# The last chunk of a fused attention and mixer kernel: its twelve stores spread over three DMA queues, its last sums and products in another order

## The chip, the cores and the metric

The kernel runs on one core of a Trainium2 chip. The metric is the device time of one execution in microseconds. Three runs of the kernel before took 278.12 us in the median (277.63 to 278.62).

The engines are named as in the profile: PE (TensorE, matmuls), DVE (VectorE), ACT (ScalarE), POOL (GpSimd) and SP (SyncE). DMAs are issued from three queues, those of SP, ACT and POOL. The profile lists SP's and ACT's as hardware queues (q1 and q10) and POOL's as a software queue (q0).

## The reference

Two layers follow each other. First comes attention with random features, for 8 batches, 8 heads, 576 positions and head size 64; then a mixer of tokens and channels with a residual:

```python
def phi(x):
    proj = np.einsum('bhsd,md->bhsm', x, omega)
    h = proj - np.sum(x * x, axis=-1, keepdims=True) / 2.0
    h = h - np.max(h, axis=-1, keepdims=True)
    return np.exp(h) / np.sqrt(m)
num = np.einsum('bhsm,bhmd->bhsd', q_p, np.einsum('bhsm,bhsd->bhmd', k_p, v))
den = np.einsum('bhsm,bhm->bhs', q_p, np.sum(k_p, axis=2))[..., None] + 1e-06
attn = num / den                                   # then laid out as x[8, 576, 512]

h = np.maximum(x.transpose(0, 2, 1) @ w_tok1, 0.0) @ w_tok2
u = x + h.transpose(0, 2, 1)
out = u + np.maximum(u @ w_ch1, 0.0) @ w_ch2       # float32, [8, 576, 512]
```

The change touches only the end of the last line, for the last 64 positions of all batches.

## The kernel before

**Work.** Each batch has 576 positions. The first 512 are handled batch by batch: attention, the token mixing, then the channel mixing (`channel_mix`, chunks 0 to 7). The 64 positions that are left of each of the 8 batches, 512 rows together, form one more chunk, chunk 8, the tail chunk. It is the last that runs through the channel mixing.

**The channel mixing of the late chunks.** Chunks 6 to 8 compute both matrix products by a scheme of seven block products instead of eight. In `channel_in_fast` the first product (`w_ch1`) is made in three parts p = 0, 1, 2 of seven small products each (line 1062). ACT and DVE copy or add partial results and apply the relu into the tile `r3`. In `channel_out_fast` the second product (`w_ch2`) follows. DVE first forms eight sums of pieces of `r3` (line 315, into the tile `S` or in place into `r3`): four steps, S1 to S4, each for a wide piece of 1024 columns and a narrow one of 512. S3 needs S1, S2 needs S1, and S4 needs S2.

**The tail chunk's last products.** There are seven products P0 to P6 (line 974), and in the tail chunk each comes in two halves, written P0.0 and P0.1 here. A half is 6 matmuls of 128 x 256. The halves accumulate in PSUM banks X (P0, P2, P4, P6, one after the other in the same bank), Y (P1) and Z (P3, then P5). After most of them DVE reads the bank and adds it to a float32 output tile `o` (the function `read`, line 963, 128 x 256): after P0 a partial sum `sA`, after P1 the finished block "11", after P2 a partial sum `s2`, after P4 `s3` and the finished block "22", after P5 the block "12" and after P6 the block "21". A product that continues in a bank waits until DVE has read it: P2 waits for `sA`, P4 for `s2`, P6 for `s3`. P2 needs the sums S2, P3 needs S1, P4 needs S3, P5 needs S4 and "22".

**The stores.** Twelve DMAs (line 1008) write the tail chunk out, 1 MB in all. "11" and "22" go out in two DMAs of 128 KB each, "12" and "21" in four DMAs of 64 KB each, one for each half j of the block and each half h of the 128 partitions. A store waits for the add that finishes its block.

**What sets the order.** Every piece of work is a job with a number. The list `ORDER` is the order in which the jobs are written out, and so the order on each engine and queue; each of them then runs strictly in order. `MOVED` says on which engine or queue a job runs where it isn't the usual one (`Planner.engine`). `SLOT` gives the buffer, PSUM banks among them, that a job takes. In the tail chunk the jobs 1357 to 1364 are the eight sums, 1365 to 1392 the products and reads, and 1393 to 1404 the twelve stores: 1393 and 1394 for "11", 1395 and 1396 for "22", 1397 to 1400 for "12", 1401 to 1404 for "21".

Before the change SP issues six of these stores, ACT five and POOL one (half of "22").

Of the kernel before, what the change touches and what calls it, by code (L numbers as in the profile page):

```python
# [72 lines left out]
]  # L73
SLOT = (
    "00010203010320452601510723430620153041112620702502331263741135100701332152700363111752044635171215600104072136510401273621522140701320204361"
# [1 line left out]
    "04517322047005311612173514326237325013271134051111260072314032102412101175140312243734612076123001643271034026270212356407101203501602731203"  # L77
    "51000022303022110212325010035101304703570352241401503037324610116010571232406752300411653700131615312021032420156003302110112723154023060401"
    "72243026013120507143162205711104320671127624033130231407036010103311726102015136272205122012050023132563724453203712351036012200643312721212"
    "0457020201451136170210500120741161405003243500210211470641212204101161421164200510731016272126007230400257120607120111261370211660"  # L80
)
MOVED = {
43: "ACT", 51: "ACT", 54: "ACT", 56: "ACT", 59: "ACT", 62: "ACT", 65: "ACT", 66: "ACT", 75: "DVE", 86: "ACT", 106: "DVE", 120: "ACT", 135: "DVE", 137:
# [4 lines left out]
"ACT", 737: "DVE", 752: "DVE", 758: "DVE", 762: "DVE", 768: "DVE", 862: "ACT", 865: "ACT", 876: "DVE", 879: "ACT", 901: "DVE", 909: "DVE", 911: "DVE",  # L88
915: "DVE", 979: "ACT", 1013: "ACT", 1027: "DVE", 1057: "DVE", 1069: "DVE", 1078: "DVE", 1088: "DVE", 1090: "DVE", 1098: "ACT", 1099: "ACT", 1100:
"ACT", 1101: "ACT", 1111: "DVE", 1154: "DVE", 1160: "ACT", 1174: "ACT", 1191: "ACT", 1205: "DVE", 1211: "ACT", 1216: "DVE", 1237: "DVE", 1246: "DVE",  # L90
1251: "DVE", 1265: "DVE", 1276: "ACT", 1278: "ACT", 1315: "DVE", 1331: "DVE", 1345: "DVE", 1353: "ACT", 1354: "ACT", 1355: "ACT", 1356: "ACT", 1393:
"ACT", 1394: "SP", 1395: "SP", 1397: "ACT", 1398: "SP", 1399: "ACT", 1400: "SP",
}


# [1139 lines left out]
```

## Time and profile before

| | |
|---|---|
| median of three runs | 278.12 us |
| the profiled execution | 278.79 us |
| its span (first to last instruction) | 277.0 us |
| PE busy | 264.7 us, 96% of the span |
| DVE busy | 225.5 us, 81% |
| ACT busy | 177.4 us, 64% |
| POOL busy | 83.4 us, 30% |

The profile is of one execution. All places in time are microseconds from the start of its span. A row of a timeline has the start, the busy time, the engine, the line, what is written and read, and a count; a "q" behind an engine marks its queue or sequencer, and in brackets stands how long the engine was idle before and what ended that.

Of a DMA the profile has three things: the stretch in which its queue issues it, the time from the start of that to the landing of the data, and the share of time in which the core's 16 DMA engines moved packets.

### The profile page before, as it was taken

To read this page: it belongs to the slowest core of one execution; us is meant where nothing else is said; L and a number is where in the kernel's file an instruction comes from. 1 tells how busy PE (TensorE), PEld (TensorE's weight loads), DVE (VectorE), ACT (ScalarE), POOL (GpSimd) and SP (SyncE) were. 2 spreads that over 40 slices of the span, in tenths; PEclk is the share of its full clock that TensorE was granted. 3 is DMA by queue.
4 is the path that set the end of the run, shared out by engine and by line. 5 is a ranking of instruction groups with operands and counts; after the bars stand their busy time and mean duration, and the time that the engine had idled before them with its cause. 6 is when DMAs were issued, how large, how long until landed. Compare 5 with 4: busy or idle time off the path is not lost.

```text
span 277.0 us, 6623 instructions
## 1 busy us (share of the span) xinstructions
PE 264.7 (96%) x2621; PEld 178.9 (65%) x2621; DVE 225.5 (81%) x475; ACT 177.4 (64%) x426; POOL 83.4 (30%) x107
## 2 busy tenths in 40 slices
PE   5679999999999999999999999999999999999993
PEld 2647546454656665666578546774597788888882
DVE  1588857748788978997899779999899979879892
ACT  2699998159896488845766485888777244352620
POOL 8497664006430490180007910332400000000000
PEclk9559999999999999999999999999999999999999
DMA  6999999998999989799909993970430151030215
GB/s 164 186 206 194 185 187 187 205 261 150 212 221 109 204 184 151 159 207 194 254 12 168 222 227 26 180 168 2 87 106 1 21 151 78 0 123 32 102 54 150
DMA packets 80623, 39.69 MB, mean 143 GB/s; under 512 B 63984, under 2 KB 76144, under 8 KB 80400
## 3 DMA queue, kind: packets, MB, share of 16 engines
q0 software_dynamic: 31696, 17.61, 43.7%
q1 hardware_dynamic: 47984, 19.70, 31.7%
q10 hardware_dynamic: 912, 1.97, 2.1%
q8 instruction: 20, 0.33, 0.5%
q14 instruction: 11, 0.09, 0.1%
HBM read 35.95 MB, written 16.52 MB: 189 GB/s over the span
## 4 chain that ended last, share of the span: by engine, by line
PE 83%; DMA 8%; DVE 3%; POOL 2%; ACT 1%; issue 1%; POOLq 0%
PE bank L974 26%; PE bank L1129 21%; PE bank L1062 10%; PE bank L829 5%; PE bank L842 4%; PE bank L1164 4%; DMA k<-in_k_dram 3%; PE bank L759 3%; DMA wc<-in_moe_w_ch_dram 3%; DMA r<-in_k_dram 3%; PE bank L792 3%; PE bank L713 2%; PE bank L725 2%; ACT qp L566 1%; DVE u L845 1%
## 5 line engine op out<-in xcount | busy, mean ns | idle before, releaser
L1129 PE MATMUL bank<-uT,wc 128*128 128x512 f16 x280 | 67.4, 379 | 0.1
L310 ACT ACTIVATE r<-bank 128x512 f16<-128x512 f32 (+1 forms) x73 | 42.5, 609 | 25.5 <-PE bank L1129 11.6
L315 POOL TENSOR_TENSOR vs<-v,vs 128x512 f16<-128x512 f16 x25 | 26.3, 1059 | 69.4 <-DVE vs L740 46.2
L1129 PEld LDWEIGHTS <-wc 128*128 128x128 f16 x280 | 25.6, 98 | 25.1 <-issue 0.6
L974 PEld LDWEIGHTS <-r 128*128 128x128 f16 x384 | 37.2, 98 | 6.4 <-issue 0.6
L566 ACT ACTIVATE qp<-bank 128x512 f16<-128x512 f32 x64 | 36.5, 623 | 7.6 <-PE bank L725 5.3
L566 ACT ACTIVATE kp<-bank 128x512 f16<-128x512 f32 x64 | 35.6, 613 | 6.1 <-PE bank L713 6.0
L736 DVE TENSOR_REDUCE km<-kp 128x8 f16<-128x1024 f16 x32 | 38.1, 1198 | 1.5 <-ACT kp L566 1.5
L974 PEld LDWEIGHTS <-S 128*128 128x128 f16 x288 | 27.4, 98 | 4.9 <-issue 1.3
L812 ACT ACTIVATE x<-bank,rc 128x64 f16<-128x64 f32 x120 | 26.9, 332 | 2.4 <-DVE rc L801 2.2
L312 DVE TENSOR_SCALAR r<-bank 128x512 f16<-128x512 f32 (+1 forms) x35 | 23.5, 672 | 4.3 <-PE bank L1062 2.2
L974 PE MATMUL bank<-wc,r 128*128 128x256 f16 x192 | 23.7, 273 | 0.0
L974 PE MATMUL bank<-T,r 128*128 128x256 f16 x192 | 23.6, 273 | 0.2 <-DVE o L963 0.2
L974 PE MATMUL bank<-T,S 128*128 128x256 f16 x192 | 23.6, 273 | 0.0
L1008 POOL DMA_DIRECT2D out_dram<-o x1 | 0.7, 667 | 74.0 <-issue 74.0
L963 DVE TENSOR_TENSOR o<-u,bank 128x512 f32<-128x512 f16 x28 | 18.9, 677 | 1.3 <-PE bank L974 0.9
L809 DVE TENSOR_TENSOR x<-bank,rc 128x320 f16<-128x320 f32 x40 | 18.7, 480 | 0.7
L845 DVE TENSOR_TENSOR u<-x,bank 128x512 f16<-128x512 f16 x28 | 17.6, 680 | 1.6 <-PE bank L842 1.4
L792 PEld LDWEIGHTS <-qp 128*128 128x128 f16 x256 | 13.6, 99 | 6.3 <-issue 0.6
L801 DVE RECIPROCAL rc<-bank 128x5 f32<-128x5 f32 x64 | 10.3, 180 | 8.8 <-PE bank L794 8.6
L315 POOL TENSOR_TENSOR vbd<-vt,vbd 128x512 f16<-128x512 f16 x6 | 6.3, 1051 | 36.8 <-DVE vbd L649 18.4
L963 DVE TENSOR_TENSOR o<-o,bank 128x512 f32<-128x512 f32 (+1 forms) x25 | 15.2, 612 | 2.3 <-PE bank L974 2.0
(151 smaller groups left out, 494.7 us busy)
## 6 DMA issues: line engine op xcount, KB each, us to landing
out_dram<-o SPq DMA_DIRECT2D x12, 512.0 KB, 3.1
q<-in_q_dram POOLq DMA_DIRECT2D x6, 576.0 KB, 8.2
wc<-in_moe_w_ch_dram POOLq DMA_DIRECT2D x4, 768.0 KB, 9.8
k<-in_k_dram POOLq DMA_DIRECT2D x6, 512.0 KB, 7.6
v<-in_v_dram POOLq DMA_DIRECT2D x6, 512.0 KB, 9.4
r<-in_q_dram POOLq DMA_DIRECT2D x4, 288.0 KB, 6.8
v<-in_v_dram POOLq DMA_DIRECT2D x4, 256.0 KB, 9.4
out_dram<-o SPq DMA_DIRECT2D x4, 256.0 KB, 4.2
```

Source lines behind the costliest of these rows:

```text
L310: nc.scalar.activation(out=out, in_=in_, func=AF.Relu)
L312: nc.vector.tensor_relu(out=out, in_=in_)
L315: (nc.gpsimd if eng == "POOL" else nc.vector).tensor_tensor(**kw)
L566: nc.scalar.activation(out=out, in_=in_, func=AF.Exp, bias=0.0, scale=1.0)
L736: nc.vector.reduce_max(out=t_km[place("km", (b, hp))], in_=kpv, axis=AX.X)
L792: nc.tensor.matmul(ps[:, k, j * 65 : (j + 1) * 65], st, s[:, i, 0 : D + 1], start=True, stop=True)
L812: nc.scalar.activation(out=to[:, j], in_=ps[:, j], func=AF.Copy, scale=rc_of()[:, j : j + 1])
L845: nc.vector.tensor_tensor(out=t_u[place("u", b)][:, j, :], in0=t_x[place("x", b)][:, j, :], in1=bank(n), op=ALU.add)
L963: nc.vector.tensor_tensor(out=o, in0=a, in1=ps, op=ALU.add)
L974: nc.tensor.matmul(ps[:, j * DH : (j + 1) * DH], a[:, cb, j * P : (j + 1) * P], w[:, cb, :], start=(bank_of(b, j0) not in held and j == j0 ...
L1062: nc.tensor.matmul(ps[:, 2 * P * t : 2 * P * t + 2 * P], a_[:, k, cb * P : (cb + 1) * P], m[:, :, k, :], start=(begin and t == 0 and k == ...
L1129: nc.tensor.matmul(ps, wc1[:, db, cb * P : (cb + 1) * P], moving(db), start=(db == 0), stop=(db == ND - 1))
```

## The change

Three tables are changed, and nothing else: the last 90 or so entries of `ORDER`, the last digits of `SLOT`, and some entries of `MOVED`. The computation stays the same.

```diff
-"ACT", 1394: "SP", 1395: "SP", 1397: "ACT", 1398: "SP", 1399: "ACT", 1400: "SP",
+1251: "DVE", ..., 1343: "DVE", 1353: "ACT", 1354: "ACT", 1355: "ACT", 1393: "POOL", 1394:
+"SP", 1395: "ACT", 1397: "POOL", 1400: "POOL", 1401: "ACT", 1402: "SP", 1403: "POOL", 1404: "SP",
```

**Stores.** POOL issues five of the twelve stores instead of one. On POOL's queue (`o_133` holds the blocks "11" and "12", `o_132` the blocks "21" and "22"; 64x2x256 is a store of 128 KB, 64x256 one of 64 KB):

```order
 L315 TENSOR_TENSOR vbd_114<-vt_93,vbd_114 128x8x64
+L1008 DMA out_dram<-o_132 64x256
 L1008 DMA out_dram<-o_132 64x2x256
+L1008 DMA out_dram<-o_133 64x2x256
+L1008 DMA out_dram<-o_133 64x256 x2
 L1230 UNCONDITIONAL_BRANCH
```

POOL's first store now is half of the first finished half of "21"; halves of "22" and "11" follow, and it ends with one store of each half of "12", the last of all among them.

SP's queue has four of the stores instead of six:

```order
 L1015 DMA out_dram<-o_132 128x1024
+L1008 DMA out_dram<-o_132 64x256
 L1008 DMA out_dram<-o_133 64x2x256
-L1008 DMA out_dram<-o_132 64x2x256
-L1008 DMA out_dram<-o_132 64x256 x2
-L1008 DMA out_dram<-o_133 64x256 x2
+L1008 DMA out_dram<-o_132 64x256
+L1008 DMA out_dram<-o_133 64x256
 L1230 UNCONDITIONAL_BRANCH
```

What moved there: the store of half of "22" went to ACT, and one store of "12" to POOL. ACT's queue has three instead of five: "22", then one of "21", then one of "12".

**Products.** The fourteen half products stand in another order. On PE, from P3 on, one row for each half product of 6 matmuls (`S_71` as the second operand marks P2, P3 and P5, `r30_130` the others; before, in the order P3.0, P3.1, P1.1, P2.0, P2.1, P1.0, P4.0, P4.1):

```order
L974 MATMUL bank2_65<-T_72,S_71 128x256
L974 MATMUL bank1_64<-T_72,S_71 128x256
L974 MATMUL bank6_69<-wc2_81,r30_130 128x256
L974 MATMUL bank7_70<-T_72,S_71 128x256
L974 MATMUL bank3_66<-T_72,S_71 128x256
L974 MATMUL bank6_69<-wc2_81,r30_130 128x256
L974 MATMUL bank7_70<-T_72,r30_130 128x256
L974 MATMUL bank3_66<-T_72,r30_130 128x256
```

After those come P6.0, P6.1, P5.1 and P5.0. Now, in the order P3.1, P3.0, P2.1, P2.0, P4.1, P4.0, P1.0:

```order
L974 MATMUL bank7_70<-T_72,S_71 128x256
L974 MATMUL bank1_64<-T_72,S_71 128x256
L974 MATMUL bank2_65<-T_72,S_71 128x256
L974 MATMUL bank3_66<-T_72,S_71 128x256
L974 MATMUL bank2_65<-T_72,r30_130 128x256
L974 MATMUL bank3_66<-T_72,r30_130 128x256
L974 MATMUL bank6_69<-wc2_81,r30_130 128x256
```

After those come P6.1, P6.0, P1.1, P5.0 and P5.1. So P1, which stood between P3 and P2 and between P2 and P4, is behind P4 with one half and behind P6 with the other, and P4 follows P2 directly.

**Sums.** DVE's order changes with it. Its rows from the narrow S1 on, before:

```order
L315 TENSOR_TENSOR S<-r_130 128x512
L315 TENSOR_TENSOR r_130<-r_130 128x4x256
L315 TENSOR_TENSOR S<-S,r_130 128x512
L963 TENSOR_TENSOR o_133<-ut,bank_66 128x256
L963 TENSOR_TENSOR o_133<-ut,bank_70 128x256
L315 TENSOR_TENSOR S<-S,r_130 128x1024
L315 TENSOR_TENSOR S<-r_130,S 128x1024
L315 TENSOR_TENSOR r_130<-r_130 128x2x256
L963 TENSOR_TENSOR o_133<-o_133,bank_69 128x256
```

Now:

```order
L312 TENSOR_SCALAR r_130<-r_130 128x2x256
L315 TENSOR_TENSOR S<-r_130 128x512
L315 TENSOR_TENSOR S<-S,r_130 128x1024
L315 TENSOR_TENSOR S<-S,r_130 128x512
L963 TENSOR_TENSOR o_133<-ut,bank_65 128x256
L315 TENSOR_TENSOR r_130<-r_130 128x2x256
L963 TENSOR_TENSOR o_133<-ut,bank_66 128x256
L315 TENSOR_TENSOR r_130<-r_130 128x4x256
L963 TENSOR_TENSOR o_133<-ut,bank_65 128x256
L963 TENSOR_TENSOR o_133<-ut,bank_66 128x256
L315 TENSOR_TENSOR S<-r_130,S 128x1024
```

Both pieces of S2 now come before the `sA` reads, the wide S3 stands between the two `sA` reads and the two `s2` reads, and S4 stands behind the `s2` reads. A relu of 512 columns (job 1356, line 312) came to DVE from ACT. Earlier in the tail chunk two more jobs changed sides: the relu of part 2 of the first product (job 1343, 512 columns from PSUM) went from ACT to DVE, and a copy of 512 columns (job 1345) from DVE to ACT. ACT's last three relus come in the order of parts 2, 1, 0, while PE makes the products that they read in the order 0, 1, 2.

More of the change, by code (lines that the diff above doesn't have):

```diff
@@ L79 @@
     "72243026013120507143162205711104320671127624033130231407036010103311726102015136272205122012050023132563724453203712351036012200643312721212"
-    "0457020201451136170210500120741161405003243500210211470641212204101161421164200510731016272126007230400257120607120111261370211660"
+    "0457020201451136170210500120741161405003243500210211470641212204101161421164200510731016272126007230400257120607120111261230711606"
 )
@@ L90 @@
 "ACT", 1101: "ACT", 1111: "DVE", 1154: "DVE", 1160: "ACT", 1174: "ACT", 1191: "ACT", 1205: "DVE", 1211: "ACT", 1216: "DVE", 1237: "DVE", 1246: "DVE",
-1251: "DVE", 1265: "DVE", 1276: "ACT", 1278: "ACT", 1315: "DVE", 1331: "DVE", 1345: "DVE", 1353: "ACT", 1354: "ACT", 1355: "ACT", 1356: "ACT", 1393:
-"ACT", 1394: "SP", 1395: "SP", 1397: "ACT", 1398: "SP", 1399: "ACT", 1400: "SP",
+1251: "DVE", 1265: "DVE", 1276: "ACT", 1278: "ACT", 1315: "DVE", 1331: "DVE", 1343: "DVE", 1353: "ACT", 1354: "ACT", 1355: "ACT", 1393: "POOL", 1394:
+"SP", 1395: "ACT", 1397: "POOL", 1400: "POOL", 1401: "ACT", 1402: "SP", 1403: "POOL", 1404: "SP",
 }
```

8 rows, old and new, of the table ORDER are left out of this document.

## The prediction

> **What bounds the kernel now.** I read the page first, then the chain of waits over the last microseconds, then the timelines of the engines and queues there, and last the transfers.
>
> ```profile
> span 277.0 us, 6623 instructions
> PE 83%; DMA 8%; DVE 3%; POOL 2%; ACT 1%; issue 1%; POOLq 0%
> ```
>
> The span is PE's to 83%. But the change starts only some 20 us before the end, so what counts is what ends last there. The chain of waits of the last 27 us closes with these pieces (start, length, what):
>
> ```profile
> 262.96 1.31 PE bank L1062 x12
> 264.27 8.02 PE bank L974 x72
> 272.28 0.02 issue
> 272.31 0.42 DVE o L963
> ```
>
> PE runs without a break until 272.3, and one add follows until 272.73. The span goes on for 4.3 us more, and these belong to the stores. On their queues:
>
> ```profile
> 270.57 0.61 SPq L1008 DMA_DIRECT2D out_dram<-o  x1
> 271.13 0.67 POOL L1008 DMA_DIRECT2D out_dram<-o  x1 [74.01 <-issue]
> 272.57 0.68 SPq L1008 DMA_DIRECT2D out_dram<-o  x1
> 272.86 0.59 ACTq L1008 DMA_DIRECT2D out_dram<-o  x1
> 273.35 0.55 SPq L1008 DMA_DIRECT2D out_dram<-o  x1
> 273.55 0.64 ACTq L1008 DMA_DIRECT2D out_dram<-o  x1
> ```
>
> Their landings, from the DMA view of three windows (KB each, us from issue to landing): the SP and the POOL store of "22", issued at 270.57 and 271.13, and ACT's last, issued at 273.55.
>
> ```profile
> out_dram<-o SPq DMA_DIRECT2D x1, 128.0 KB, 2.5
> out_dram<-o POOLq DMA_DIRECT2D x1, 128.0 KB, 3.0
> out_dram<-o ACTq DMA_DIRECT2D x1, 64.0 KB, 2.1
> ```
>
> The block that is finished at 272.73 is issued only at 273.35 and 273.55, because SP and ACT are still busy with earlier stores: the last issue is 0.82 us late. It lands at 273.55 + 2.1 = 275.7. SP's queue has waited for that landing for 1.7 us, and it then goes through its remaining semaphores:
>
> ```profile
> SPq L1230 <- DMA out_dram<-o: 1.7, 1, 1.7
> L1230 SPq EVENT_SEMAPHORE  x11: 17/28/28, 273.9 to 277.0; - x11
> ```
>
> So 277.0 - 275.7 = 1.3 us stand behind the last landing whatever lands last. The end is set by PE's last product, the add, the queues, the transfer, and this rest. The transfers themselves are not free either. Windows of one microsecond (their length, then each engine's busy time, the clock, the share of the DMA engines, GB/s):
>
> ```profile
> 270.00:271.00 1.00, 1.00 (x10) 0.77 (x9) 0.85 (x4) 0.00 (x0) 0.00 (x0) 1.00 0.83 203
> 271.00:272.00 1.00, 1.00 (x12) 0.88 (x10) 0.77 (x2) 0.00 (x0) 0.67 (x1) 1.00 0.28 86
> 272.00:273.00 1.00, 0.27 (x3) 0.00 (x0) 0.50 (x2) 0.00 (x0) 0.00 (x0) 1.00 0.84 194
> 273.00:274.00 1.00, 0.00 (x0) 0.00 (x0) 0.00 (x0) 0.00 (x0) 0.00 (x0) 1.00 0.92 258
> 274.00:275.00 1.00, 0.00 (x0) 0.00 (x0) 0.00 (x0) 0.00 (x0) 0.00 (x0) 1.00 0.87 259
> 275.00:277.00 2.00, 0.00 (x0) 0.00 (x0) 0.00 (x0) 0.00 (x0) 0.00 (x0) 1.00 0.09 25
> ```
>
> From 272 to 275 the DMA engines are busy to 84 to 92%. They stop 0.09 x 2.0 = 0.2 us past 275.0, and the landing is seen about 0.5 us later.
>
> **Part 1: sums and products.** PE does the same 84 half-product matmuls, DVE nearly the same work. These rows price it:
>
> ```profile
> 264.10 1.47 PE L974 MATMUL bank<-T,S 128*128 128x256 f16 x12
> 268.03 2.93 PE L974 MATMUL bank<-T,r 128*128 128x256 f16 x24
> 270.80 1.47 PE L974 MATMUL bank<-wc,S 128*128 128x256 f16 x12
> 261.85 0.68 DVE L1075 TENSOR_TENSOR r<-r,bank 128x512 f16<-128x512 f32 x1
> 263.57 0.69 DVE L315 TENSOR_TENSOR r<-r 128x1024 f16<-128x1024 f16 x1
> 264.17 0.42 DVE L315 TENSOR_TENSOR S<-S,r 128x512 f16<-128x512 f16 x1
> 264.51 0.74 DVE L963 TENSOR_TENSOR o<-ut,bank 128x256 f32<-128x256 f16 x2
> L312 DVE TENSOR_SCALAR r<-r 128x1024 f16<-128x1024 f16 x2 | 0.8, 422 | 0.0
> ```
>
> 72 matmuls in 8.02 us against 12 in 1.31 leave 8.02 - 6 x 1.31 = 0.16 us of waiting. It lies in the 24 matmuls from 268.03 to 270.80: 2.77 us, where 24 at the pace of the chain's 1.31/12 take 2.62. There P6 waits for the `s3` adds. In the new order P1.0 stands between P4 and P6, which gives DVE 0.65 us more, so I take these 0.15 us as gone.
>
> What could be late next is P4, which now follows P2 directly and waits for `s2`. On DVE a wide sum takes its slot for 264.17 - 263.57 = 0.60 us, a narrow one for 0.34, an add for 0.74 - 0.41 = 0.33, the relu that came to it about half of its 1024-column row and a little, 0.25. I lay the new order out from the last add of the first product, which I leave at 261.85 (its slot 0.60). S1 wide starts at 262.45, the relu at 263.05, S1 narrow at 263.34, S2 at 263.67 and 264.27, `sA` at 264.60, S3 narrow at 264.94, `sA` at 265.27, S3 wide from 265.60 to 266.29. PE, at 0.655 us for a half, starts P3.1 at 264.10 as before, P2.1 at 265.41, P2.0 at 266.07, and wants to start P4.1 at 266.72. P2.1 is done shortly before 266.27; the `s2` add then takes 0.41, to 266.68. P4.1 so waits for 0.0 to 0.1 us. The bounds are 0, and 0.6 if each add had to wait for a whole wide sum. I take 0.05, since S3 wide ends within 0.02 us of the point where the add can start. P6 and P5 then find their adds done with 0.1 us and more to spare. Sum of this part: -0.15 + 0.05 = -0.1 us; the last add ends at about 272.6.
>
> The jobs that changed sides cost nothing on the path: the relu of part 2 takes 0.60 us on DVE from about 257.3, and the add that it delays is needed only by a product at 259.7. The copy on ACT starts behind a relu that ends at 257.53 and is done before its reader's time, 258.9. ACT's last three relus end up to 0.9 us later, since ACT starts with the part that PE makes last, at about 265.9; their readers, P1.0 and S4, come at 267.2 or later. The rows of the cover:
>
> ```profile
> 256.47 1.06 ACT L310 ACTIVATE r<-r 128x1024 f16<-128x1024 f16 x1 [2.50 <-DVE r L1075]
> 258.86 0.60 PE L1062 MATMUL bank<-uTt,wc 128*128 128x256 f16 x4
> 259.74 1.47 PE L974 MATMUL bank<-wc,S 128*128 128x256 f16 x12
> 263.43 1.57 ACT L310 ACTIVATE r<-bank 128x512 f16<-128x512 f32 x3 [0.23 <-PE bank L1062]
> ```
>
> **Part 2: the queues of SP and ACT.** With seven stores instead of eleven, they no longer run late. SP's last store comes at 272.6 behind one that starts at about 272.1 and takes 0.6, so at about 272.75. At 2.1 to 2.5 us it lands by 275.3. Alone that would be worth up to 0.4 us.
>
> **Part 3: POOL's queue.** Five issues of 0.67 us. What POOL costs is seen here:
>
> ```profile
> L1008 POOLq EVENT_SEMAPHORE  x1: 76414/76414/76414, 194.2 to 194.2; - x1
> 270.13 0.42 DVE L963 TENSOR_TENSOR o<-o,bank 128x256 f32<-128x256 f32 x1
> L371 POOL DMA_DIRECT2D vt<-in_v_dram x16 | 10.8, 680 | 0.3 <-POOL vbd L315 0.3
> L390 POOL DMA_DIRECT2D k<-in_k_dram x12 | 10.2, 854 | 0.1
> ```
>
> "22" was finished at 270.55, POOL's wait ended at 194.2 + 76.4 = 270.6, and its store started at 271.13, where SP's started at 270.57: POOL wakes up 0.55 us later. But where stores or loads queue up, it issues one behind the other: 28 loads at 0.68 to 0.85 us with 0.4 us of idle time in all. So I start the five at 270.6, 271.3, 271.9, 272.6 and, whichever is later, 273.3 (five at 0.67) or 272.6 + 0.55 = 273.15. From there to landing 2.1 us at least (ACT's last, on engines that run empty) and 3.0 at most (POOL's row, twice the size). I take 2.4, nearer to ACT's because the size and the empty engines are the same and 0.5 of POOL's 3.0 is what separates it from SP's 2.5 on the same block. The last store then lands at 275.7, between 275.3 and 276.3.
>
> The Trainium skill, in "DMA: Bandwidth & Descriptors", section "Anatomy of one DMA — SWDGE (gpsimd) path", fits a POOL DMA with 2.0 us and its bytes over 436 GB/s. As an estimate by that page, 64 KB take 2.15 us and the last landing is at 275.4, 0.3 us earlier; the trace's 128 KB, at 3.0 against the page's 2.3, speak for the later value.
>
> **Part 4: the transfers.** Before, "11" was stored at 268.7, and its quarter of the megabyte had moved by 271.1 (the first two windows). Now "11" is finished near 271.3, and the whole megabyte moves from the first store on. That one is issued at about 270.05, and 1.3 us pass before its packets run (the store of 270.57 brings only a share of 0.28 to the window up to 272). The windows from 272 to 275 move 194, 258 and 259 KB, together 0.71 MB, at a mean share of 0.88, so full engines move 0.27 MB per us. 1.05 MB take 3.9 us: from 271.4 to 275.3, and 0.5 us to the landing give 275.8; what one queue alone leaves unused up to 272 comes on top, some 0.2 at most.
>
> **Sum.** Part 3 says 275.7, part 4 275.8 to 276.0, before it was 275.7. I take 275.8, +0.1 us: the queues' gain and the 0.1 us of part 1 are used up by the engines and by POOL's late start. The profiled execution would have a span of 277.1 instead of 277.0. It took 278.79, 0.7 us above the median of 278.12, so I put the difference on the median: 278.2 us. A measurement of this kernel can tell about 0.3%, 0.8 us, from no change.
>
> **Rivals.**
>
> *The queues are all that counts (gain).* For it: the last issue is 0.82 us late on two queues that are full from 270.6 on. Against it: the shares of 0.84 to 0.92. If the engines keep up and POOL lands in 2.1 us, the last landing is at 275.25, 0.45 us earlier: 277.7. For 0.3% it would have to be at 274.85, 1.7 us behind POOL's last start, which no row of a store shows. The Trainium skill, in "Perfetto Trace Analysis", section "DMA Optimizations", says for this gain that spreading DMAs over sync, scalar and GpSimd may help where issuing them is the bottleneck and not the transfer; by the shares above it is both.
>
> *POOL wakes up anew for each store (slower).* Each of the five would then cost 0.55 + 0.67 = 1.22 us, the fifth would start at 270.6 + 4 x 1.22 = 275.5, land at 277.9 with 2.4, and the time would be 2.2 us above now: 280.3. For it: in this trace no POOL DMA that waits for DVE stands right behind another; the 28 loads had little to wait for. Against it: a queue that is already busy when its wait ends shows no gap anywhere. It decides from a last start later than 274.1 (274.1 + 2.4 + 1.3 = 277.8, 0.8 above now).
>
> *POOL's own end sets the span (a little slower).* Its queue's closing instruction ran until 271.1 + 3.5 = 274.6, half a microsecond past the landing of its only store:
>
> ```profile
> L1230 POOLq DRAIN  x3: 51/93/3512, 271.1 to 276.7; - x3
> ```
>
> If that came 3.5 - 0.7 = 2.8 us behind the last issue, it would end at 274.0 + 2.8 = 276.8, where SP's chain reaches POOL at 276.3 now: 0.5 us more, 278.6.
>
> **Chances.** My forecast with its neighbours (the sum, the smaller gain, POOL's end), all within 0.3%: 0.70. POOL waking anew, in full or in good part: 0.17; other ways to lose 0.8 us (DVE's order holding PE up at several places, transfers that disturb one another): 0.06. A gain of more than 0.8 us: 0.07. So faster 0.07, same 0.70, slower 0.23. The range goes from 277.5 (the first rival with part 1's 0.15 us in full) to 279.4, where POOL pays about half of its wakes.
>
> **What would show it.** Right: PE without waits above 0.1 us from 264 to 272, the last add at 272.5 to 272.7, SP's last store issued before 272.9, POOL's five starts 0.6 to 0.75 us apart, DMA shares of 0.85 and more from 272 to 275, a last landing at 275.5 to 276.1 that is POOL's. Wrong: gaps of 0.5 us between POOL's stores, or engines that run empty before 274.5.

## The result and the profile after

The changed kernel takes 278.82 us in the median of 13 runs (278.4 to 279.63), the kernel before 278.17 us in 13 runs beside it. The ratio is 1.0020, with a 95% interval of 1.0012 to 1.0028: it is slower by 0.56 us, 0.33 to 0.78 us. The forecast was 0.1 us.

The profiled execution of the changed kernel has a span of 276.9 us, shorter than that of before. That is no gain of the change: here the whole program runs a microsecond earlier long before the change begins. POOL's long wait ahead of its first store starts at 193.1 in this trace and at 194.2 in that of before, and the start of P3 has the same lead. So the two traces are compared from the start of P3 on. Of the changed kernel, the page's first line and rows of the timelines of PE and DVE (P3 and P2; P4; the last add):

```profile
span 276.9 us, 6620 instructions
263.06 2.78 PE L974 MATMUL bank<-T,S 128*128 128x256 f16 x24
265.74 1.47 PE L974 MATMUL bank<-T,r 128*128 128x256 f16 x12
271.18 0.42 DVE L963 TENSOR_TENSOR o<-o,bank 128x256 f32<-128x256 f32 x1 [0.23 <-PE bank L974]
```

| from the start of P3 | before | after |
|---|---|---|
| start of P3 | 264.10 | 263.06 |
| to the last add's end | 8.63 us | 8.55 us |
| from there to the last landing | 2.95 us | 4.06 us |
| from there to the end of the span | 1.34 us | 1.24 us |
| start of P3 to the end | 12.92 us | 13.85 us |

So the compute part became 0.08 us shorter, and the way from the last add to the last landing 1.11 us longer. The stores of the changed kernel, each by its row on SP's and on ACT's queue, POOL's five together:

```profile
269.05 0.56 SPq L1008 DMA_DIRECT2D out_dram<-o  x1
270.32 0.65 SPq L1008 DMA_DIRECT2D out_dram<-o  x1
271.03 0.67 SPq L1008 DMA_DIRECT2D out_dram<-o  x1
271.79 1.47 SPq L1008 DMA_DIRECT2D out_dram<-o  x1
270.98 0.50 ACTq L1008 DMA_DIRECT2D out_dram<-o  x1
269.61 2.88 POOL L1008 DMA_DIRECT2D out_dram<-o  x5 [73.53 <-DVE o L963]
L1008 POOL DMA_DIRECT2D out_dram<-o x5: 544/589/642, 269.6 to 271.9; - x5
```

The queues do what the change wanted of them: the last add ends at 271.60, SP's last issue starts at 271.79 and POOL's at 271.9. The landings are another matter. The DMA view of the last stretch of the changed kernel, all twelve stores (KB each, median us from issue to landing), and then of the window that holds only the two last:

```profile
out_dram<-o POOLq DMA_DIRECT2D x2, 128.0 KB, 3.8
out_dram<-o SPq DMA_DIRECT2D x3, 64.0 KB, 3.9
out_dram<-o POOLq DMA_DIRECT2D x3, 64.0 KB, 3.5
out_dram<-o ACTq DMA_DIRECT2D x1, 128.0 KB, 2.9
out_dram<-o ACTq DMA_DIRECT2D x2, 64.0 KB, 4.1
out_dram<-o SPq DMA_DIRECT2D x1, 128.0 KB, 4.5
...
out_dram<-o SPq DMA_DIRECT2D x1, 64.0 KB, 3.9
out_dram<-o POOLq DMA_DIRECT2D x1, 64.0 KB, 3.5
```

Before, a 64 KB store took 2.7 us in the median and the last one 2.1. Now the medians of the three queues are 3.5 to 4.1, and the last to land is SP's: 271.79 + 3.9 = 275.7, behind POOL's at 275.4. SP's last issue itself took 1.47 us instead of the usual 0.6. The windows of the changed kernel, with the columns of those before:

```profile
270.00:271.00 1.00, 1.00 (x11) 0.78 (x8) 0.71 (x2) 0.00 (x0) 1.00 (x3) 1.00 0.56 131
271.00:272.00 1.00, 0.14 (x2) 0.00 (x0) 0.42 (x1) 0.00 (x0) 1.00 (x3) 1.00 0.74 165
272.00:273.00 1.00, 0.00 (x0) 0.00 (x0) 0.00 (x0) 0.00 (x0) 0.48 (x1) 1.00 0.91 218
273.00:274.00 1.00, 0.00 (x0) 0.00 (x0) 0.00 (x0) 0.00 (x0) 0.00 (x0) 1.00 0.97 301
274.00:275.00 1.00, 0.00 (x0) 0.00 (x0) 0.00 (x0) 0.00 (x0) 0.00 (x0) 1.00 0.73 231
```

The DMA engines moved 131 and 165 GB/s in the first two windows, and in the last they were at 0.73 while SP's last stores were still out.

### The profile page after: what moved, and what is told of

It reads as the page before. It is cut to its first block, busy times and chain, and to the rows that moved or that the text cites. A ratio compares the mean times of both kernels' runs of the same rounds, so it can differ in the third digit from the quotient of the medians.

```text
span 276.9 us, 6620 instructions
## 1 busy us (share of the span) xinstructions
PE 265.2 (96%) x2621; PEld 179.2 (65%) x2621; DVE 225.6 (81%) x476; ACT 176.5 (64%) x425; POOL 85.5 (31%) x111
## 4 chain that ended last, share of the span: by engine, by line
PE 55%; issue 27%; DMA 8%; POOL 4%; DVE 2%; ACT 1%; POOLq 0%
PE bank L1129 20%; PE bank L974 13%; PE bank L829 4%; PE bank L1164 4%; PE bank L842 3%; DMA k<-in_k_dram 3%; DMA r<-in_q_dram 3%; DMA wc<-in_moe_w_ch_dram 2%; PE bank L759 2%; PE bank L792 2%; PE bank L725 2%; PE bank L713 2%; ACT qp L566 1%; DVE u L845 1%; POOL vs L315 1%
## 5 line engine op out<-in xcount | busy, mean ns | idle before, releaser
L312 DVE TENSOR_SCALAR r<-bank 128x512 f16<-128x512 f32 (+1 forms) x36 | 24.3, 674 | 4.3 <-PE bank L1062 2.2
L1008 POOL DMA_DIRECT2D out_dram<-o x5 | 2.9, 587 | 73.5 <-DVE o L963 73.5
```

What stands on the lines that cost most here:

```text
L312: nc.vector.tensor_relu(out=out, in_=in_)
```

## The experiments

Each kernel was timed beside the kernel before on the same chip and profiled once. "P3 to end" is the time from the start of P3 to the end of the span in its profile, free of what happens earlier in the program. A line number can be a few off from that of before.

| kernel | ratio to before (95% interval) | P3 to end | last add to last landing | of it: until that store's issue + issue to landing | last landing to end |
|---|---|---|---|---|---|
| before | 1 | 12.92 us | 2.95 us | 0.82 + 2.13 | 1.34 |
| the change | 1.0020 (1.0012 to 1.0028) | 13.85 | 4.06 | 0.19 + 3.88 | 1.24 |
| e1: new order, old queues | 1.0003 (0.9990 to 1.0017) | 13.34 | 3.61 | 1.07 + 2.54 | 1.19 |
| e2: old order, new queues | 1.0027 (1.0013 to 1.0040) | 13.66 | 3.87 | 0.20 + 3.67 | 1.16 |
| e3: the change without "11" | 0.9989 (0.9978 to 1.0000) | 12.90 | 2.96 | 0.29 + 2.66 | 1.40 |
| e5: old order, no POOL | 0.9987 (0.9970 to 1.0004) | 12.93 | 3.01 | 0.80 + 2.21 | 1.29 |
| e6: old order, three early on POOL | 0.9975 (0.9965 to 0.9985) | 12.63 | 2.96 | 0.14 + 2.82 | 1.04 |
| e7: old order, "21" joined | 0.9986 (0.9974 to 0.9999) | 12.63 | 2.95 | 0.40 + 2.55 | 1.05 |
| e8: "21" joined, no POOL | 0.9963 (0.9951 to 0.9976) | 12.34 | 2.73 | 0.34 + 2.39 | 0.99 |
| e9: old order, three late on POOL | 0.9996 (0.9983 to 1.0009) | 13.09 | 3.42 | 0.14 + 3.28 | 1.04 |
| e10: old order, five early on POOL | 0.9997 (0.9985 to 1.0009) | 13.15 | 3.34 | 0.03 + 3.31 | 1.17 |

From the start of P3 to the last add's end it is 8.63 us in every kernel with the old order and 8.54 or 8.55 with the new one, so nearly all that differs in "P3 to end" lies behind the last add. The last store to land is one of SP's or ACT's in all of them but e3, where it is POOL's.

The order of the kernels is nearly the same by the ratio and by "P3 to end". But the timed differences from before are on average 0.3 us lower than those of the profiles (e8: -1.03 us against -0.58; the change: +0.56 against +0.93). One profile of before stands against all of them, so its tail was probably a short one; this is left open, and a difference of 0.3 us between two profiles is to be read with care.

### Order or queues

The first two kernels each make one half of the change. Edit of e1, in the tables of the changed kernel:

```diff
-... 1393: "POOL", 1394: "SP", 1395: "ACT", 1397: "POOL", 1400: "POOL", 1401: "ACT", 1402: "SP", 1403: "POOL", 1404: "SP",
+... 1393: "ACT", 1394: "SP", 1395: "SP", 1397: "ACT", 1398: "SP", 1399: "ACT", 1400: "SP",
```

> The changed order of sums and products, but the twelve stores on the queues of before (SP six, ACT five, POOL one). In the trace of the changed kernel 5.3 us pass from the last add's end to the end of the span, before 4.3 us. Theory A, the whole megabyte meets in the last 5 us because "11" is finished at the end: the tail stays at 5.0 us or more and the time is 0.5 us or more above before. Theory B, POOL's five stores are what is slow: the tail is back at 4.3 to 4.6 us and the time within 0.2 us of before, or 0.1 us under it, since the last add comes 0.1 us earlier.

e2 has the reverse edit in the kernel before.

> The order of before, with "11" stored at 268.7, but the stores on the queues of the change (POOL five). Theory A: 768 KB are left for the end as before, the tail is 4.3 to 4.6 us and the time within 0.2 us of before. Theory B: POOL's stores slow the transfers here as well, the tail is 4.9 us or more and the time 0.5 us above before.

Measured: from the last add's end to the end of the span 4.80 us in e1 and 5.03 us in e2, P3 to end 0.42 and 0.74 us above before, timed +0.1 and +0.75 us. The queues are the greater half, and alone they cost as much as the whole change within the intervals: theory B for the most part. But theory A is not empty: in the profile the new order alone brings the last landing 0.57 us later behind the start of P3 (e1). What the new order leaves for the end can be counted in the trace. These are the packets from the last add's end to 276, of before, e2, e1 and the changed kernel:

```profile
DMA packets 682, 0.63 MB, mean 193 GB/s; under 512 B 144, under 2 KB 656, under 8 KB 682
DMA packets 539, 0.63 MB, mean 156 GB/s; under 512 B 145, under 2 KB 465, under 8 KB 539
DMA packets 863, 0.82 MB, mean 186 GB/s; under 512 B 160, under 2 KB 831, under 8 KB 863
DMA packets 678, 0.83 MB, mean 188 GB/s; under 512 B 160, under 2 KB 582, under 8 KB 678
```

With the old order 0.63 MB are left behind the last add, with the new one 0.2 MB more. At the 0.27 MB per us of the prediction that is 0.7 us, and e1's last landing comes 0.66 us later behind its last add than before. The two halves of the change don't add up, 0.42 + 0.74 against 0.93. The windows of e2:

```profile
272.00:273.00 1.00, 0.00 (x0) 0.00 (x0) 0.00 (x0) 0.00 (x0) 0.66 (x2) 1.00 0.89 228
273.00:274.00 1.00, 0.00 (x0) 0.00 (x0) 0.00 (x0) 0.00 (x0) 0.00 (x0) 1.00 0.77 222
274.00:275.00 1.00, 0.00 (x0) 0.00 (x0) 0.00 (x0) 0.00 (x0) 0.00 (x0) 0.52 0.54 168
```

The same 0.63 MB as before are left for the end here, but the engines drop to 0.77 and 0.54 with all stores issued by 272.8. So in e2 it isn't that they have more to do than before: with five stores on POOL part of the engines' time goes unused while stores wait.

### Is it the amount at the end

> The changed kernel without the two stores of the block "11" (256 KB of the tail chunk are left unwritten). If the DMA engines' work sets the last landing (both theories), a quarter less to move at 0.27 MB per us takes 0.7 to 0.9 us off: the tail is 4.4 to 4.6 us and the time at or below before. If the last store's own way through its queue sets it, the tail stays at 5.0 us or more.

```diff
 ...
+                        if need == "11":
+                            return
 ...
```

Without the 256 KB the span from P3 is 0.95 us shorter than with them, 12.90 us, a little more than the 0.7 to 0.9 us expected. The last store's way depends on what else is under way. Which part of that counts this kernel can't tell: one of the two stores left out was POOL's, so there is less to move and one store less on POOL at once.

### The late issue of before

Four kernels with the order of before ask what the 0.82 us are worth by which SP and ACT issued the last block late. The first tried to halve the number of issues of "12" and "21" by one store for both halves of the partitions:

```diff
+                        if need in ("12", "21"):
+                            if (need, j0, h) not in (("21", 0, 0), ("21", 1, 1), ("12", 1, 1), ("12", 0, 0)):
+                                return
+                            q = ...
+                            q.dma_start(out=out[4 * i + 2 * j0 : 4 * i + 2 * j0 + 2, SM:S, cols], in_=t_o[place("o", (c, i))][:, j0, cols])
+                            return
```

> The kernel before with each pair of 64 KB stores of "12" and "21" made into one store of 128 KB over all 128 partitions: eight stores instead of twelve, SP four, ACT three, POOL one. If the two queues that issue late were worth something, the last store starts 0.05 us behind the last add instead of 0.82 us; at 2.3 to 2.6 us to landing the tail is 3.7 to 4.0 us and the time 0.3 to 0.6 us below before. If the engines' work alone sets the landing, the tail stays at 4.2 us or more.

It went the wrong way by 10 us: ratio 1.0362 (1.0345 to 1.0379). Its windows, of four microseconds each:

```profile
274.00:278.00 4.00, 0.00 (x0) 0.00 (x0) 0.00 (x0) 0.00 (x0) 0.00 (x0) 0.67 0.13 42
278.00:282.00 4.00, 0.00 (x0) 0.00 (x0) 0.00 (x0) 0.00 (x0) 0.00 (x0) 0.50 0.14 49
```

These stores run at a share of 0.13 to 0.14, which is 2 of 16 engines, at 42 to 49 GB/s. On the side of the output such a store is 2 blocks of 64 rows. The Trainium skill, in "DMA: Bandwidth & Descriptors", section "Why a DMA increments its semaphore by 16 and not by 1", says that a DMA is spread over as many engines, 16 at most, as divide its slowest dimension on both sides; for a slowest dimension of 2 that gives 2, as the share shows. About the late issue this kernel says nothing. The next three ask again.

e5 gives POOL's store to ACT (`1396: "ACT"`).

> The order of before, POOL's one store of "22" given to ACT: SP six, ACT six, POOL none. Theory C, POOL's stores delay those of SP and ACT on the shared engines (with five of them the tail, from the last add's end to the span's end, went from 4.3 to 5.0 us): without any the tail is 4.2 us or less and the time 0 to 0.2 us below before. Theory D, it is the late issue on two queues that counts: one more issue of 0.65 us on ACT makes the tail 4.6 to 4.9 us and the time 0.3 us or more above before.

e6 gives two stores of "21" to POOL (`1402: "POOL", 1403: "POOL"`).

> The order of before, POOL three: its store of "22" and two of the four stores of "21", so that POOL has nothing of the last block and SP and ACT can issue that at once. Theory C: between before and the five-store kernel, tail 4.5 to 4.8 us, time 0.2 to 0.4 us above before. Theory D: the last issue comes 0.05 us behind the last add instead of 0.82 us, tail 3.7 to 4.0 us, time 0.3 us or more below before.

e7 joins the halves j of "21", and so keeps the 64 partitions:

```diff
 ...
+                        if need == "21":
+                            if j0 == 0:
+                                return
+                            js = slice(0, 2)
 ...
```

> The kernel before with the four stores of "21" joined into two of 128 KB, each over 64 partitions and both halves j: two issues fewer, the same bytes, all queues as before. Theory D: the last issue is no longer late, tail 3.8 to 4.0 us, time 0.3 us or more below before. Theory E, the engines' work sets the last landing and half of "21" now starts 0.5 us later: tail 4.3 to 4.5 us, time within 0.2 us of before or above.

e8 is e7 with the queues of e5.

> The joined stores of "21" and no store on POOL: SP five, ACT five. Theory C with D: tail 3.7 to 4.0 us, 0.3 to 0.5 us below before, the best of the four. Theory E: tail 4.2 us or more, time within 0.2 us of before.

Measured, P3 to end: e5 12.93, e6 12.63, e7 12.63, e8 12.34 us; timed, 0.4, 0.7, 0.4 and 1.0 us below before. Theory D, by which the late issue counts, fits the times of e6 and e7 and the 4.0 us that their tails take, but the profiles show another reason. Their last store is issued 0.68 and 0.42 us sooner behind the last add than before and takes 0.69 and 0.42 us longer to land, so the last landing comes at the same place, 2.96 and 2.95 us behind the last add against 2.95. For the landing that is theory E, whose range for the tail, 4.3 to 4.5 us, is still missed: with the same bytes left, an earlier issue alone brought the last landing no nearer. The 0.3 us of both profiles stand behind the last landing. There SP waits for the semaphores of the stores one after the other, in the same order of semaphores in every kernel and one each 0.06 us. Such waits behind the last landing, in before and in e6:

```profile
L1230 SPq EVENT_SEMAPHORE  x8: 28/28/28, 275.7 to 276.1; - x8
L1229 SPq EVENT_SEMAPHORE  x3: 27/28/28, 274.9 to 275.0; - x3
```

Before, the last store to land stands early in this order, and eight waits are left, its own among them; in e6 and e7 three are left, in e8 two. Five waits less are 0.3 us. No edit aimed at this. That e6 and e7 are also faster in time, by 0.7 and 0.4 us, is more than that in e6, and what the rest comes from is not shown.

e5 issues its last store 0.80 us behind the last add, as late as before, with one store more on ACT. Its tail of 4.30 us lies between the ranges of C and D and decides neither. e8 is the best: it is faster than both kernels, by 0.37% (0.24 to 0.49%) than before. Of the 0.58 us that its profile gains, 0.36 are the shorter rest behind the last landing; the landing itself comes 0.22 us sooner behind the last add. Its last store and its windows:

```profile
272.31 0.64 ACTq L1011 DMA_DIRECT2D out_dram<-o  x1
272.00:273.00 1.00, 0.00 (x0) 0.00 (x0) 0.00 (x0) 0.00 (x0) 0.00 (x0) 1.00 0.94 287
273.00:274.00 1.00, 0.00 (x0) 0.00 (x0) 0.00 (x0) 0.00 (x0) 0.00 (x0) 1.00 0.93 287
274.00:275.00 1.00, 0.00 (x0) 0.00 (x0) 0.00 (x0) 0.00 (x0) 0.00 (x0) 0.97 0.10 31
```

The engines move 287 GB/s here, where in e2 with five stores on POOL they moved 228 and 222. A third queue as such does not slow them, as the same two windows of e6 with its three early stores on POOL show:

```profile
272.00:273.00 1.00, 0.00 (x0) 0.00 (x0) 0.00 (x0) 0.00 (x0) 0.10 (x1) 1.00 0.96 254
273.00:274.00 1.00, 0.00 (x0) 0.00 (x0) 0.00 (x0) 0.00 (x0) 0.00 (x0) 1.00 0.96 293
```

### How many on POOL, or which

e6 has three stores on POOL and gains; e2 has five and loses. Two more kernels separate the number from the place. e9 (three, two of them of the last block: `1397: "POOL", 1400: "POOL"`):

> The order of before and three stores on POOL as in e6, but other ones: its store of "22" and two of the four stores of "12", the last block. Theory F, what costs is that POOL carries the last block beside SP and ACT (not how many stores it has): from the start of P3 to the span's end 13.3 us or more (before 12.92, e6 12.63, e2 13.66), time 0.3 to 0.7 us above before. Theory G, the number of POOL's stores costs: 12.6 to 12.9 us as in e6, time 0 to 0.7 us below before.

e10 (five, none of the last block: `1393`, `1401`, `1402`, `1403: "POOL"`):

> The order of before and five stores on POOL as in the changed kernel, but early ones: one each of "11" and "22", three of "21"; the last block is left to SP and ACT. Theory F: 12.6 to 12.9 us from the start of P3 to the end, time 0 to 0.7 us below before. Theory G: 13.4 us or more as in e2, time 0.5 us above before.

Both end in the middle, at 13.09 and 13.15 us and about 0.1 us from before in time. Neither theory holds alone: to the last landing three late ones cost 0.46 us against three early ones, and five early ones 0.39 us against three. Five don't stay early, either: they queue up on POOL, and e10's fifth is issued at 271.8, when the last add ends. How long the last store takes to land is a measure of this only among kernels that issue it about equally soon, since one that is issued late meets less of the others. Where the issue comes 0.03 to 0.34 us behind the last add, it takes 2.4 us with none on POOL (e8), 2.8 with three early ones (e6), 3.3 with three late or five early ones (e9, e10), 3.7 in e2 and 3.9 in the changed kernel. The 2.1 to 2.5 us of before, e5, e7 and e1 belong to issues 0.4 to 1.1 us late. The more of POOL's stores are under way beside it, the longer the last one takes.

Why they hold it up is not shown. The DMA view counts packets by queue; in the last stretch of the changed kernel:

```profile
DMA packets 880, 1.05 MB, mean 117 GB/s; under 512 B 192, under 2 KB 768, under 8 KB 880
q0 software_dynamic: 192, 0.46, 18.6%
q1 hardware_dynamic: 384, 0.33, 14.0%
q10 hardware_dynamic: 304, 0.26, 11.0%
```

The 192 packets below 512 bytes are sixteen for each of the twelve stores. That leaves 112 of POOL's 192, as many as the view has above 2 KB, for 0.46 MB, and 576 of SP's and ACT's for 0.59 MB, so a packet of POOL's carries 4.1 KB, four times as much as one of theirs. If the engines take turns by packet, SP's and ACT's stores get the smaller part while POOL's last, and are left to finish at the end. That would not yet leave engines idle while stores are out, as the shares of 0.77 and 0.54 in e2 show them; for that they must be unevenly loaded. The trace has no view by engine, but its records of the landings fit: a store's semaphore is raised in sixteen steps, and from the first to the last step of the last store to land 0.22 us pass before, 0.97 us in the changed kernel and 1.38 us in e2 (274.44 to 275.82). So part of e2's store was through more than a microsecond ahead of the rest. What makes the load uneven stays open. No kernel with smaller packets on POOL was tried.

## Why the prediction was right and where it was wrong

**Right in sign, size short.** Slower by 0.1 us was forecast, 0.56 us came, inside the range and inside the 0.3% that were called no change. That this band held is in part luck: in the profile, from the start of P3 on, the change costs 0.93 us, more than the 0.8 us that the band is wide (one profile against one), and the term behind it was missed. Of the signs that were named, those of PE, of the last add and of SP's issue came, and POOL's starts were 0.54 to 0.62 us apart; the shares of the DMA engines were 0.74, 0.91 and 0.97 instead of 0.85 and more, and the last landing came 0.6 us behind its range and was SP's.

**Part 1, right.** -0.1 us forecast, -0.08 measured from the start of P3 to the last add's end. P4 follows the four half products of P3 and P2 at 265.74, 2.68 us after P3's start, where 24 matmuls take 2.62: a wait of 0.06 against 0.05. The waits ahead of P6 are gone. The jobs that changed sides cost nothing that can be seen.

**Part 2, wrong.** SP's last issue starts 0.19 us behind the last add, 0.15 was forecast. But its landing was put at 2.1 to 2.5 us from rows beside which POOL had one store, and that one landed at 274.1, 0.6 us behind the last issue; with five of them it took 3.9, and with five in the old order 3.7 (e2). This is the step that failed most: the durations of SP's and ACT's stores were carried over as if POOL's queue had no part in them.

**Part 3, right in the issue, wrong in the landing.** POOL wakes up once: its first store starts at 269.61, 0.59 us behind the add, and the five follow each other in 2.88 us, 0.58 each, so the last starts 0.3 us sooner than forecast. The rival that it wakes up anew each time is out for the change, where POOL never runs dry. The landing took 3.5 us instead of 2.4, above the bound of 3.0.

**Part 4, right in kind, too small.** It named the engines as the limit, and took them as full from the first packet: 3.9 us for 1.05 MB. The windows show 0.56 and 0.74 at the start and 0.73 at the end. In the frame of before the last landing was put at 275.8; measured, it lies 12.6 us behind P3's start, at 276.7. Those 0.9 us are the missing term. The work itself was sized right: the shares of the three queues, 18.6 + 14.0 + 11.0% of the nine microseconds of that view, are 3.9 us. From the first packet to the last, 270.3 to 275.1, it was stretched over 4.9 us, because the engines were not full.

**The rest.** The end came 1.24 us behind the last landing, 1.3 forecast. That this rest is the same whatever lands last was wrong: it goes from 0.99 to 1.40 us, by how many of SP's waits follow and, in e3, also by POOL's own end. In the change POOL's own end cost next to nothing: its closing instruction ran 4.24 us from 271.9, to 276.1, where SP got through at about the same time.

```profile
L1230 POOLq DRAIN  x3: 51/102/4238, 271.9 to 276.6; - x3
```

Only SP's late landing hid it. Counted from the start of P3, POOL was through 0.9 us later than SP's chain reached it before, so with SP in time this rival would by itself have cost more than the 0.5 us that it was given.

**The rivals.** A gain from the queues exists in time, as e6 and e8 show, but not with this change. In the profiles a good part of it lies behind the last landing, and only e8, with no store on POOL and fewer of them, brings the last landing itself forward.

## What to carry to other kernels

Where a kernel ends in stores, count for the last block both when its queue is free to issue it and what else is in flight on the DMA engines; a third queue shortens the first and can lengthen the second by more. In e2 the last issue came 0.62 us sooner and its landing took 1.54 us longer. A duration from issue to landing belongs to the mix of transfers in which it was measured and shouldn't be carried into another mix. Fewer and larger stores on two queues, with the last block free to go at once, were worth 0.37% here, where the change, with five of the twelve on a third queue, cost 0.2%. Part of the 0.37% came with the order in which SP waits for the stores at the end, so look there too before a gain is put down to the transfers.

## What the hardware showed that was not expected

- The last store from SP or ACT takes 2.1 to 3.9 us from issue to landing for the same 64 KB, by what is under way beside it, POOL's stores above all; even its issue can stretch, from 0.6 to 1.47 us.
- A store of 128 KB whose output side is 2 blocks of 64 rows ran at 0.13 to 0.14 of the DMA engines' time and 42 to 49 GB/s; four of them cost 10 us.
- POOL's first store starts 0.55 to 0.6 us behind what it waited for if POOL was idle for long, and 0.3 us behind the add after a short wait (e9: adds that end at 271.49 and 272.15, starts at 271.79 and 272.45). Behind another DMA of its own there was no gap to see in the changed kernel.
- At the end SP waits for each store's semaphore in turn, 0.06 us each, so the time from the last landing to the end went from 0.99 to 1.40 us with which store landed last and with POOL's own end.
